# Order of the second scores, the first row sums and v's last cast in batch 0

## The chip, the cores and the metric

The kernel runs on one core of a Trainium2 chip. Its five engines work side by side, each through its own list of instructions in order, and wait for each other by semaphores: TensorE (PE, with its weight loads as PEld), VectorE (DVE), ScalarE (ACT), GpSimd (POOL) and SyncE (SP). The metric is the device time of one execution in microseconds (us), as the median of several runs.

## The reference

```python
k_proj = np.einsum('ks,bhsd->bhkd', E, k)
v_proj = np.einsum('ks,bhsd->bhkd', F, v)
scores = scale * np.matmul(q, k_proj.transpose(0, 1, 3, 2))
scores = scores - np.max(scores, axis=-1, keepdims=True)
attn = np.exp(scores)
attn = attn / (np.sum(attn, axis=-1, keepdims=True) + 1e-09)
attn_out = np.matmul(attn, v_proj).astype(np.float32)
...
x = np.ascontiguousarray(attn_out.transpose(0, 2, 1, 3)).reshape(B * S, H * D)
h1 = x @ w1
h2 = x @ w2
g = np.maximum(h1, h2)
return (g @ w_out).astype(np.float32)
```

There are 8 batches of 8 heads, 1024 positions and 64 dimensions a head. Keys and values are projected from 1024 positions to 64 by E and F, attention runs against these 64, and a layer of 512 to 1024 to 512 with the larger of two products follows on the 8192 rows.

## The kernel before

The kernel takes batch by batch, and each batch in two halves. The heads of a batch form two groups, g=0 (heads 0 to 3) and g=1 (heads 4 to 7), and the positions two halves, j=0 and j=1. A pair (g, j) is one unit of attention: 512 positions of four heads.

The softmax has no maximum; it goes by Exp, row sums, and an inverse made by ACT as the Exp of minus the Ln of the sums. For each unit there are these steps, written as functions in the code:

- `step_sc` (L376): the scores on PE (L340) into a tile of two PSUM banks, and Exp of all 1024 columns on ACT (L380) into `ex`.
- `step_dn` (L382): the row sums, as matmuls of `ex` with ones on PE (L352), into the first half of the same two banks that held the scores; then Ln on ACT (L388) from these banks into `ld`.
- `step_inv` (L425): Exp of minus `ld` on ACT (L427), in place, and a DMA of 8 KB on SP's queue that keeps one row of each inverse in `checked` (L396). `checked` is looked at once, near the end of the kernel, to see whether the sums lay in the range for which this way is exact enough.
- `step_at` (L430): the values on PE (L352), `ex` against the projected v, and two products with the inverse on DVE (L443) that write `xt`, the rows of x, transposed.

`step_kv` (L183) projects k or v. For v it does two heads at a time: 16 matmuls (L195) for each two heads, then one copy of all into `vp` as 16-bit numbers (L207), by DVE or by the engine that is passed as `copy`. With `between` a step is put between the first two heads and the next two.

PSUM has eight banks. Four are single, taken in turn by `mm_bank` (L65). The other four are two tiles of two banks each under the tag `att`, taken in turn by `att_banks` (L71): whoever asks for the third such tile takes the first one's buffer again, and waits until all readers of it are done.

The schedule is manual: each engine's order is the order of the calls. In batch 0, which has no earlier batch to hide its attention behind, the order is written out line by line (L956 to L1005). The part around the change, L984 to L994, before it:

```python
    step_sc(t, 1, 0)
    step_kv(t, 0, 2, "v")
    step_kv(t, 2, 4, "v")
    step_dn(t, 1, 0)
    step_sc(t, 1, 1)
    step_at(t, 0, 0)
    step_at(t, 0, 1)
    step_inv(t, 1, 0)
    step_kv(t, 4, 8, "v", True, copy=nc.scalar.copy, between=lambda: step_dn(t, 1, 1))
    step_inv(t, 1, 1)
    att_banks()
```

The call of `step_kv` for heads 4 to 7 asks for an `att` tile (its fifth argument), puts the second row sums and their Ln between heads 4, 5 and heads 6, 7, and has ACT do the cast. The bare `att_banks()` passes over one buffer in the turn. Behind these lines come `step_wd` (L540: w1 - w2 on DVE, written to `wd_sb`), the values of (1, 0) and (1, 1), and the first matmuls of the up product (`up_slots`, L525), which read `wd_sb` and `xt`; then a transpose of w2 (`step_w2t`, L557) into an `att` tile. The products of `step_at(t, 0, ·)`, which stand earlier, read the inverses of g=0, made well before, and use single banks. The arrival of v is in four DMAs of two heads each.

Of the kernel before, what the change touches and what calls it, by code (L numbers as in the profile page):

```python
# [19 lines left out]
def kernel(  # L20
# [12 lines left out]
    nc = tc.nc  # L33
# [31 lines left out]
    def mm_bank(dtype=FP32, n=None):  # L65
        if n is None:
            n = turn.pop(0)
            turn.append(n)
        return ps.tile([128, 512 if dtype == FP32 else 1024], dtype, tag=f"mm{n}", name="mm_ps")

    def att_banks(dtype=FP32):  # L71
        return ps.tile(
            [128, 2, 512 if dtype == FP32 else 1024], dtype, tag="att", bufs=2, name="att_ps"
        )
# [108 lines left out]
    def step_kv(t, h0=0, h1=H, which="kv", att=False, dma=False, copy=nc.vector.tensor_copy, between=None):  # L183
        kv_ps = att_banks()[:, 0, :] if att else mm_bank(n=0 if dma else None)
        n = (h1 - h0) * D
        both = which == "v"
        nh = 2 if both else h1 - h0
        for h in range(0, h1 - h0, nh):
            if h and between is not None:
                between()  # L190
            for c in range(NC):
                for w in which:
                    i = "kv".index(w)
                    for r in range(2) if both else (i,):
                        nc.tensor.matmul(  # L195
                            out=kv_ps[r * KP : (r + 1) * KP, h * D : (h + nh) * D],
                            lhsT=eft[i][:, c, :],
                            rhs=t[w][:, h0 + h : h0 + h + nh, c, :],
                            start=(c == 0), stop=(c == NC - 1),
                        )  # L200
        zd = lambda ap: ap.rearrange("p (h d z) -> p h z d", d=D // 2, z=2)
        if "k" in which:
            eng = nc.vector.tensor_copy if which == "k" or dma else nc.scalar.copy
            kp = t["kp"][:, h0:h1]
            eng(out=kp[:, :, 0, :], in_=kv_ps[0:KP, 0:n].rearrange("p (h d) -> p h d", d=D))
        if both:
            copy(out=t["vp"][:, h0:h1], in_=zd(kv_ps[:, 0:n]))  # L207
        elif "v" in which:
            def finish_v():
                nc.vector.tensor_copy(out=t["vp"][KP:128, h0:h1], in_=zd(kv_ps[KP:128, 0:n]))  # L210
                if dma:
                    nc.vector.tensor_copy(out=kp[:, :, 1, :], in_=kp[:, :, 0, :])
                    step_kpt_dma(t)
                else:
                    step_vp(t, h0, h1)

            if att:
                return finish_v
            finish_v()


    def step_vp(t, h0=0, h1=H):
        fl = lambda ap: ap[:, h0:h1].rearrange("p h z d -> p (h z d)")
        nc.vector.tensor_copy(out=fl(t["vp"][0:KP]), in_=fl(t["vp"][KP:128]))
# [71 lines left out]
    def step_kpt_dma(t):  # L296
        nc.sync.dma_start_transpose(
            out=t["kpt"], in_=t["kp"].rearrange("p h r d -> p (h r d)")
        )
# [33 lines left out]
    def score(t, g, j, banks):  # L333
        for h in range(2):
            for o in range(2):
                for e in range(2):
                    head = 4 * g + 2 * h + e
                    for s in range(2):
                        pos = D * (o ^ e) + s * Z
                        nc.tensor.matmul(  # L340
                            out=banks[e][pos : pos + Z, h * W : (h + 1) * W],
                            lhsT=kpt_of(t, head, o)[:, s * Z : (s + 1) * Z],
                            rhs=t["qt"][o * D : (o + 1) * D, head, j * W : (j + 1) * W],
                            start=True, stop=True,
                        )
        t["ex", g, j] = soft.tile([128, 2, HALF], FP16, tag="soft", name="ex_sb")
# [12 lines left out]
    def sums_into(t, g, j, dn_ps):  # L359
        tiles_into(lambda o: dn_ps[:, o, :], t["ex", g, j], lambda rows, hh: ones16[rows, 0:Z])  # L360

    def values_into(t, g, j, at_ps):
        for z in range(2):
            tiles_into(
                lambda o: at_ps[o][:, z * W : (z + 1) * W], t["ex", g, j],
                lambda rows, hh: vp_of(t, 4 * g + hh, rows, z),
            )

    def new_xt(t):
        t["xt"] = xpool.tile([128, NP2, 2, HALF], FP16, tag="xt", name="xt_sb")  # L370

    def x_out(t, g, j):
        return t["xt"][:, 2 * g : 2 * g + 2, :, j * W : (j + 1) * W]


    def step_sc(t, g, j):  # L376
        sc_ps = att_banks()
        t["ps", g, j] = sc_ps
        score(t, g, j, [sc_ps[:, e, :] for e in range(2)])
        nc.scalar.activation(out=t["ex", g, j], in_=sc_ps, func=ACTF.Exp, scale=scale)  # L380

    def step_dn(t, g, j):  # L382
        dn_ps = t.pop(("ps", g, j))[:, :, 0:W]
        sums_into(t, g, j, dn_ps)
        ld = (ppool.tile([128, 2, W], FP32, tag="pd", bufs=4, name="ld_sb") if t is tiles[0]
              else soft.tile([128, 2, W], FP32, tag="soft", name="ld_sb"))
        t["ld", g, j] = ld
        nc.scalar.activation(out=t["ld", g, j], in_=dn_ps, func=ACTF.Ln)  # L388
# [4 lines left out]
    def check(inv):  # L393
        rows = checked[4 * n_checked[0] : 4 * n_checked[0] + 4, :]
        n_checked[0] += 1
        nc.sync.dma_start(  # L396
            out=rows, in_=inv.rearrange("(a z) o w -> a z (o w)", z=Z)[:, 0, :]
        )
# [26 lines left out]
    def step_inv(t, g, j):  # L425
        ld = t["ld", g, j]
        nc.scalar.activation(out=ld, in_=ld, func=ACTF.Exp, scale=-1.0)  # L427
        check(ld)

    def step_at(t, g, j, att=False, between=None):  # L430
        if "xt" not in t:
            new_xt(t)
        ld = t.pop(("ld", g, j))
        if att:
            both = att_banks()
            at_ps = [both[:, o, :] for o in range(2)]
        else:
            at_ps = [mm_bank() for _ in range(2)]
        values_into(t, g, j, at_ps)
        for o in range(2):  # L440
            if o and between is not None:
                between()
            nc.vector.tensor_tensor(  # L443
                out=x_out(t, g, j)[:, :, o, :],
                in0=at_ps[o].rearrange("q (z n) -> q z n", z=2),
                in1=ld[:, o, None, :].broadcast_to([128, 2, W]),
                op=ALU.mult,
            )
# [507 lines left out]
    t = tiles[0]  # L956
# [27 lines left out]
    step_sc(t, 1, 0)  # L984
    step_kv(t, 0, 2, "v")
    step_kv(t, 2, 4, "v")
    step_dn(t, 1, 0)
    step_sc(t, 1, 1)
    step_at(t, 0, 0)
    step_at(t, 0, 1)  # L990
    step_inv(t, 1, 0)
    step_kv(t, 4, 8, "v", True, copy=nc.scalar.copy, between=lambda: step_dn(t, 1, 1))
    step_inv(t, 1, 1)
    att_banks()  # L994
    for f0 in (0, 128):
# [85 lines left out]
    t = tiles[1]  # L1081
# [29 lines left out]
    t = tiles[2]  # L1111
# [8 lines left out]
    for b in range(3, B):  # L1120
        t = tiles[b]
# [242 lines left out]
```

## Time and profile before

| | us |
|---|---|
| median of 3 runs | 319.72 (319.67 to 319.75) |
| the profiled execution | 320.29 |
| its span, first to last instruction | 318.5 |
| PE busy in the span | 311.8 (98%) |
| ACT busy in the span | 206.0 (65%) |
| DVE busy in the span | 241.1 (76%) |

The granted clock of TensorE is 1.0 throughout. In the rows of the profile the columns are: start in us from the span's start, duration in us, engine and line, operation, what it writes and reads, the shape, and the number of instructions merged in the row; in square brackets the idle time of the engine ahead of it, and what ended it. A merged row's duration goes from the first start to the last end. Matmuls overlap, so a row of PE can start a little before the row above it ends, and ACT and DVE start an instruction about 0.1 us before the one ahead of it has written its last element. A wait for several semaphores is put down to the one that came last in the profile, which need not be the one that mattered.

### The profile page before, as it was taken

To read this page: it belongs to the slowest core of one execution; us is meant where nothing else is said; L and a number is where in the kernel's file an instruction comes from. 1 tells how busy PE (TensorE), PEld (TensorE's weight loads), DVE (VectorE), ACT (ScalarE), POOL (GpSimd) and SP (SyncE) were. 2 spreads that over 40 slices of the span, in tenths; PEclk is the share of its full clock that TensorE was granted. 3 is DMA by queue.
4 is the path that set the end of the run, shared out by engine and by line. 5 is a ranking of instruction groups with operands and counts; after the bars stand their busy time and mean duration, and the time that the engine had idled before them with its cause. 6 is when DMAs were issued, how large, how long until landed. Compare 5 with 4: busy or idle time off the path is not lost.

```text
span 318.5 us, 9309 instructions
## 1 busy us (share of the span) xinstructions
PE 311.8 (98%) x3922; PEld 253.8 (80%) x3922; DVE 241.1 (76%) x442; ACT 206.0 (65%) x373; POOL 41.4 (13%) x63
## 2 busy tenths in 40 slices
PE   7999999999999999999999999999999999999996
PEld 3565588888887888788887888788887888888885
DVE  2366889887969696896969696996969696969883
ACT  2386742777776777477776777477776777765541
POOL 8259102004000300012000400030000000000000
PEclk9999999999999999999999999999999999999999
DMA  7999999999989999799999999989979131313124
GB/s 179 206 202 197 207 207 201 207 156 141 204 163 183 171 209 245 208 188 147 225 229 219 169 199 245 221 155 174 230 153 217 42 101 36 102 35 102 36 99 136
DMA packets 76684, 53.71 MB, mean 169 GB/s; under 512 B 29664, under 2 KB 76128, under 8 KB 76640
## 3 DMA queue, kind: packets, MB, share of 16 engines
q0 software_dynamic: 30688, 28.05, 56.0%
q1 hardware_dynamic: 45664, 24.85, 33.1%
q8 instruction: 31, 0.51, 0.6%
q10 hardware_dynamic: 288, 0.20, 0.2%
q14 instruction: 13, 0.11, 0.1%
HBM read 57.15 MB, written 16.78 MB: 232 GB/s over the span
## 4 chain that ended last, share of the span: by engine, by line
PE 95%; DMA 3%; ACT 1%; DVE 1%; issue 0%; POOLq 0%
PE mm_ps L838 47%; PE mm_ps L746 27%; PE mm_ps L525 4%; PE mm_ps L195 4%; PE att_ps L352 4%; PE mm_ps L340 2%; DMA k_sb<-in_k_dram 2%; PE mm_ps L634 2%; PE att_ps L237 1%; PE mm_ps L311 1%; PE mm_ps L153 1%; DMA out_dram<-o_sb 1%; PE att_ps L340 0%; DVE qt_sb L316 0%; ACT ld_sb L388 0%
## 5 line engine op out<-in xcount | busy, mean ns | idle before, releaser
L720 ACT COPY p_sb<-mm_ps 128x512 f32<-128x512 f32 x179 | 101.7, 592 | 49.2 <-PE mm_ps L746 27.3
L838 PEld LDWEIGHTS <-big 128*128 128x128 f16 x768 | 73.5, 98 | 11.8 <-issue 3.6
L838 PE MATMUL mm_ps<-T_sb,big 128*128 128x256 f16 x576 | 76.9, 273 | 0.0
L761 DVE TENSOR_TENSOR gt_sb<-mm_ps,p_sb 128x512 f16<-128x512 f32 x56 | 38.5, 688 | 43.0 <-PE mm_ps L746 41.6
L746 PE MATMUL mm_ps<-big,big 128*128 128x256 f16 x336 | 50.4, 273 | 0.0
L746 PEld LDWEIGHTS <-big 128*128 128x128 f16 x448 | 43.8, 98 | 5.1
L838 PE MATMUL mm_ps<-wo_sb,gt_sb 128*128 128x256 f16 x256 | 42.6, 273 | 0.0
L838 PEld LDWEIGHTS <-gt_sb 128*128 128x128 f16 x376 | 35.7, 98 | 6.7 <-issue 2.7
L469 ACT ACTIVATE ex_sb<-mm_ps 128x512 f16<-128x512 f32 x50 | 27.2, 597 | 18.0 <-PE mm_ps L340 12.3
L746 PEld LDWEIGHTS <-wd_sb 128*128 128x128 f16 x336 | 32.9, 98 | 3.8
L746 PE MATMUL mm_ps<-xt_sb,wd_sb 128*128 128x256 f16 x224 | 32.8, 273 | 0.0
L499 DVE TENSOR_TENSOR xt_sb<-att_ps,ld_sb 128x1024 f16<-128x1024 f32 x26 | 31.7, 1219 | 0.2
L303 POOL COPY junk<-qt_sb 1x1 f16<-1x1 f16 x6 | 2.6, 432 | 172.3 <-DMA qt_sb<-q_sb 172.3
L838 PE MATMUL mm_ps<-m_sb,xt_sb 128*128 128x256 f16 x128 | 24.4, 273 | 0.0
L869 DVE TENSOR_TENSOR o_sb<-mm_ps,p_sb 128x512 f32<-128x512 f32 x32 | 21.9, 683 | 2.8 <-ACT p_sb L898 2.0
L764 DVE TENSOR_SCALAR gt_sb<-gt_sb 128x512 f16<-128x512 f16 (+1 forms) x60 | 20.9, 348 | 2.1
L706 DVE TENSOR_TENSOR big<-gt_sb 128x1024 f16<-128x1024 f16 x32 | 21.9, 683 | 0.0
L838 PE MATMUL mm_ps<-wo_sb,big 128*128 128x256 f16 x128 | 21.5, 273 | 0.0
L807 ACT ACTIVATE gt_sb<-mm_ps 128x512 f16<-128x512 f32 x28 | 16.8, 601 | 5.7 <-PE mm_ps L746 5.7
L838 PE MATMUL mm_ps<-T_sb,gt_sb 128*128 128x256 f16 x120 | 20.3, 273 | 0.0
L838 PEld LDWEIGHTS <-xt_sb 128*128 128x128 f16 x188 | 18.3, 98 | 2.3 <-issue 0.2
L761 DVE TENSOR_TENSOR gt_sb<-p_sb 128x512 f16<-128x512 f32 x28 | 19.1, 682 | 0.6 <-ACT p_sb L720 0.6
(121 smaller groups left out, 434.8 us busy)
## 6 DMA issues: line engine op xcount, KB each, us to landing
out_dram<-o_sb SPq DMA_DIRECT2D x62, 256.0 KB
k_sb<-in_k_dram POOLq DMA_DIRECT2D x7, 1024.0 KB, 9.7
v_sb<-in_v_dram POOLq DMA_DIRECT2D x7, 1024.0 KB, 15.4
q_sb<-in_q_dram POOLq DMA_DIRECT2D x5, 1024.0 KB, 22.8
q_sb<-in_q_dram POOLq DMA_DIRECT2D x6, 512.0 KB, 15.9
big<-in_moe_w_dram POOLq DMA_DIRECT2D x12, 128.0 KB, 6.4
v_sb<-in_v_dram POOLq DMA_DIRECT2D x4, 256.0 KB, 14.0
wo_sb<-in_moe_w_out_dram POOLq DMA_DIRECT2D x1, 1024.0 KB, 10.4
```

What stands on the lines that cost most here:

```text
L195: nc.tensor.matmul(out=kv_ps[r * KP : (r + 1) * KP, h * D : (h + nh) * D], lhsT=eft[i][:, c, :], rhs=t[w][:, h0 + h : h0 + h + nh, c, :], ...
L352: nc.tensor.matmul(out=dst(r ^ (hh % 2))[hh * Z : (hh + 1) * Z, :], lhsT=weights(rows, hh), rhs=ex[rows, hh % 2, hh // 2 * W : (hh // 2 + ...
L469: nc.scalar.activation(out=t["ex", g, j][:, e, :], in_=banks[e], func=ACTF.Exp, scale=scale)
L499: nc.vector.tensor_tensor(out=x_out(t, g, j).rearrange("q z o n -> q o z n"), in0=at_ps.rearrange("q o (z n) -> q o z n", z=2), in1=ld[:, ...
L706: nc.vector.tensor_tensor(out=S(i), in0=S(0) if x is None else x, in1=y(), op=op)
L720: copy(out=x, in_=bank)
L746: nc.tensor.matmul(out=bank[:, m * W : (m + 1) * W], lhsT=w_[:, n_, (2 * d + m) * 128 : (2 * d + m + 1) * 128], rhs=a[:, n_, :], start=(n ...
L761: nc.vector.tensor_tensor(out=c_blk(j, c), in0=two(x), in1=two(y), op=ALU.add)
L764: nc.vector.tensor_scalar_max(ap, ap, 0.0)
L807: nc.scalar.activation(out=out, in_=in_, func=ACTF.Relu)
L838: nc.tensor.matmul(out=bank[i][:, 0:CH] if two_banks else bank[:, i * CH : (i + 1) * CH], lhsT=a(c)[:, i * 128 : (i + 1) * 128], rhs=w_(c) ...
L869: nc.vector.tensor_tensor(out=o_sb, in0=two(x), in1=two(y), op=ALU.add)
```

## The change

```diff
     step_sc(t, 1, 0)
     step_kv(t, 0, 2, "v")
     step_kv(t, 2, 4, "v")
+    step_sc(t, 1, 1)
     step_dn(t, 1, 0)
-    step_sc(t, 1, 1)
     step_at(t, 0, 0)
     step_at(t, 0, 1)
+    step_kv(t, 4, 8, "v", True, copy=nc.scalar.copy, between=lambda: step_dn(t, 1, 1))
     step_inv(t, 1, 0)
-    step_kv(t, 4, 8, "v", True, copy=nc.scalar.copy, between=lambda: step_dn(t, 1, 1))
     step_inv(t, 1, 1)
     att_banks()
```

The scores of (1, 1) and their Exp come ahead of the row sums of (1, 0) and their Ln. The projection of v for heads 4 to 7, with the second row sums, their Ln and the cast, comes ahead of the inverse of (1, 0), so that both inverses stand behind the cast. On PE the order turns from sums, scores, values, v, sums, v into scores, sums, values, v, sums, v. On ACT it turns from Exp(1,0), Ln(1,0), Exp(1,1), inverse(1,0), Ln(1,1), cast, inverse(1,1), into Exp(1,0), Exp(1,1), Ln(1,0), Ln(1,1), cast, inverse(1,0), inverse(1,1). DVE's order stays. SP's two DMAs to `checked` keep their order and go out when their inverses are done. The order of buffers under the tag `att` stays too: scores of (1, 0), scores of (1, 1), v, one passed over, values of (1, 0), values of (1, 1).

## The prediction

> **What bounds the kernel now.** I read the page first: busy time of each engine and the chain of waits by engine. Then I asked for PE's waits alone, from 24 us to the end.
>
> ```profile
> PE 311.8 (98%) x3922; PEld 253.8 (80%) x3922; DVE 241.1 (76%) x442; ACT 206.0 (65%) x373; POOL 41.4 (13%) x63
> PE 95%; DMA 3%; ACT 1%; DVE 1%; issue 0%; POOLq 0%
> ```
>
> ```profile
> PE mm_ps L1196 <- DMA out_dram<-o_sb: 1.2, 1, 1.2
> ```
>
> The last row is the only wait of PE after 24 us, and it stands at the very end, behind a store. So from 24 us on TensorE sets the pace without a pause: what reaches PE late before that point should be paid in full at the end of the kernel. The other engines appear on the chain for 1% each, and the question is only where. The chain in order of time, from 17 to 26 us, answers it:
>
> ```profile
> 18.84 1.20 PE mm_ps L195 x32
> 20.04 0.29 PE att_ps L352 x8
> 20.36 0.60 ACT ld_sb L388
> 20.95 0.91 ACT ex_sb L380
> 21.87 0.52 ACT ld_sb L427
> 22.38 0.50 ACT ld_sb L388
> 22.89 0.33 ACT vp_sb L207
> 23.25 0.63 PE att_ps L352 x32
> 23.89 1.83 PE mm_ps L525 x8
> ```
>
> From 20.36 to 23.25 us, 2.9 us, the chain runs through ACT, and these are the very operations that the change reorders. By this view alone one would take the inverse (L427, 0.52 us) out of the chain and promise half a microsecond. A chain names one releaser per step, however, so I laid the two engines beside each other, ACT first (start, duration):
>
> ```profile
> 18.91 1.02 ACT L380 ACTIVATE ex_sb<-att_ps 128x1024 f16<-128x1024 f32 x1 [0.57 <-PE att_ps L340]
> 20.36 0.60 ACT L388 ACTIVATE ld_sb<-att_ps 128x512 f32<-128x512 f32 x1 [0.42 <-PE att_ps L352]
> 20.85 1.02 ACT L380 ACTIVATE ex_sb<-att_ps 128x1024 f16<-128x1024 f32 x1
> 21.75 0.63 ACT L427 ACTIVATE ld_sb<-ld_sb 128x512 f32<-128x512 f32 x1
> 22.29 0.60 ACT L388 ACTIVATE ld_sb<-att_ps 128x512 f32<-128x512 f32 x1
> 22.83 0.37 ACT L207 CAST vp_sb<-att_ps 128x256 f16<-128x256 f32 x1
> 23.10 0.63 ACT L427 ACTIVATE ld_sb<-ld_sb 128x512 f32<-128x512 f32 x1
> ```
>
> ```profile
> 18.43 0.41 PE L340 MATMUL att_ps<-qt_sb,kpt_sb 64*32 64x256 f16 x16
> 18.77 1.27 PE L195 MATMUL mm_ps<-v_sb,eft 128*64 128x128 f16 x32
> 19.98 0.30 PE L352 MATMUL att_ps<-ex_sb,ones 64*32 64x256 f16 x8
> 20.09 0.41 PE L340 MATMUL att_ps<-qt_sb,kpt_sb 64*32 64x256 f16 x16
> 20.31 0.74 PE L352 MATMUL mm_ps<-ex_sb,vp_sb 64*32 64x256 f16 x32
> 21.00 0.64 PE L195 MATMUL att_ps<-v_sb,eft 128*64 128x128 f16 x16
> 21.92 0.30 PE L352 MATMUL att_ps<-ex_sb,ones 64*32 64x256 f16 x8 [0.28 <-ACT ex_sb L380]
> 22.15 0.64 PE L195 MATMUL att_ps<-v_sb,eft 128*64 128x128 f16 x16
> 23.25 0.63 PE L352 MATMUL att_ps<-ex_sb,vp_sb 64*32 64x256 f16 x32 [0.47 <-ACT vp_sb L207]
> 23.82 1.90 PE L525 MATMUL mm_ps<-xt_sb,wd_sb 128*128 128x512 f16 x8
> 25.55 0.61 PE L557 MATMUL att_ps<-ident,big 128*128 128x128 f16 x8
> ```
>
> Read across, in four links. PE's second row sums (21.92) start 0.05 us behind the end of the second Exp (20.85 + 1.02 = 21.87). The second Ln (22.29) starts 0.07 behind those sums' end (21.92 + 0.30), so the inverse at 21.75 hardly held it up. The cast of v (22.83) starts 0.04 behind the end of v's second half on PE (22.15 + 0.64 = 22.79), so the cast isn't held by ACT at all. And the values (23.25) start 0.05 behind the cast. What sets the time of the cast is therefore the row of PE work: v's first half at 21.00, the sums at 21.92, the second half at 22.15.
>
> **What the change does to this.** Nothing is added or removed: the same matmuls, activations and DMAs run in another order. There are two moves.
>
> The second move, the inverse of j=0 behind the cast (0.63 us of ACT, about 0.5 as a step between its neighbours), frees ACT between 21.75 and 22.29. I cost this at nothing: both instructions that follow it waited for PE, by the links above. Its other end needs a look, since the inverse is now late for the product on DVE that reads it:
>
> ```profile
> 23.81 1.29 DVE L443 TENSOR_TENSOR xt_sb<-att_ps,ld_sb 128x512 f16<-128x512 f32 x2
> ```
>
> This product starts 0.98 behind the cast's start (22.83), which is 0.56 behind the start of the values on PE (23.25). With the inverse behind the cast, the inverse starts 0.27 after the cast's start (as 23.10 follows 22.83), ends 0.63 later, at cast + 0.90, and with a semaphore's 0.05 the product could start at cast + 0.95. The values still decide, by 0.03 us. Were the inverse 0.1 later than this, the product would be too, and PE would not notice: its next reader of the freed bank is a transpose 1.73 us behind the start of L525 (25.55 against 23.82), while the product's pair ends at 23.81 + 1.29 = 25.10, 0.45 us ahead. The inverse also sends 8 KB to `checked` on SP's queue:
>
> ```profile
> 17.85 6.41 SPq L396 DMA_DIRECT2D checked<-ld_sb  x4
> ```
>
> SP issues nothing else between 17 and 62 us, and `checked` is read only near the end of the kernel, so the later DMA costs nothing.
>
> The first move is the one that costs. PE now runs the second scores ahead of the first sums, and so ACT's order turns from Exp, Ln, Exp into Exp, Exp, Ln. The second Exp gains, the first Ln loses. Who waits for that Ln? The `att` tag has two buffers. The first scores take one, the second scores the other, and the v projection of heads 4 to 7 asks for a third: it takes the first one's, where the first row sums have just been written, and must wait until Ln has read them. In the profile of before that wait can barely be seen: Ln ends at 20.36 + 0.60 = 20.96, v's first half starts at 21.00, and PE itself was busy until about then with the values (20.31 + 0.74 = 21.05). Now for the sum, step by step.
>
> ```profile
> 19.40 0.48 PEld L195 LDWEIGHTS <-eft 128*64 128x64 f16 x16 [0.15 <-DMA v_sb<-in_v_dram]
> 21.57 0.09 PEld L352 LDWEIGHTS <-ones 64*32 64x32 f16 x1
> ```
>
> 1. Second scores on PE. They follow v's heads 0 to 3, which end at 18.77 + 1.27 = 20.04. The change from such matmuls to small tiles is shown by the weights of the sums: loaded at 21.57, 0.07 ahead of the end of v's first half (21.64). So the scores start at 19.97 instead of 20.09.
> 2. Second Exp: scores to Exp took 18.91 - 18.43 = 0.48, so it starts at 20.45 instead of 20.85.
> 3. First Ln: an Exp of this size hands ACT on after 21.75 - 20.85 = 0.90, so Ln starts at 21.35 instead of 20.36, and ends 0.60 later, at 21.95.
> 4. v's first half: 0.05 behind it, at 22.00 instead of 21.00. Here 1.00 us is lost.
> 5. Second sums: the Exp that they waited for until 21.87 now ends at 21.47, so they follow v's first half at once, 0.57 behind its start (21.00 to 21.57): 22.57 instead of 21.92. Of the 1.00 us, the 0.35 us that PE had waited here is won back.
> 6. From there everything keeps its distances. Sums to cast is 0.91 (21.92 to 22.83), and the second Ln fits in: it starts 0.37 behind the sums and hands on 0.49 later (20.36 to 20.85), at 0.86. Cast at 23.48 instead of 22.83, values at 23.90, L525 at 24.47 instead of 23.82.
>
> The sum is 0.57 + 22.00 - 21.92 = **0.65 us later**, and by the first view it stays to the end. The profiled execution took 320.29 us, of which the span is 318.5; it would take 320.94. The median of the runs, 319.72, is 0.57 below the profiled one, and the same step on it gives 320.37 us.
>
> **Unknown costs.** Step 1 depends on a landing: PE's weights at 19.40 waited 0.15 us for heads 2 and 3 of v. A run in which these land earlier lets the second scores start up to 0.15 sooner, down to the end of the first Exp on ACT. Before, that bought nothing, as the first sums waited for that same Exp (18.91 + 1.02 = 19.93, sums at 19.98); now it goes straight into step 3. Bound below: 0.65 - 0.15 = 0.50. A later landing moves both kernels alike. Bounds above: DVE's first product starts at 20.97 and is put down to that first Ln.
>
> ```profile
> 20.97 2.49 DVE L443 TENSOR_TENSOR xt_sb<-mm_ps,ld_sb 128x512 f16<-128x512 f32 x4 [0.60 <-ACT ld_sb L388]
> 23.37 0.48 DVE L541 TENSOR_TENSOR wd_sb<-big,big 128x256 f16<-128x256 f16 x2
> ```
>
> By the code these products read the inverses of heads 0 to 3, long done, and the values, 0.66 earlier on PE (20.31); I take the latter, and the Ln (ending at 20.96) for a coincidence. If they did wait for it, they would start at 21.96, the first half of `wd_sb` would be ready at 21.96 + (23.37 - 20.97) + 0.24 (half of the pair's 0.48) = 24.60, and L525 would start there instead of 24.47: 0.78 in all. If an Exp handed on only at its end (1.02, not 0.90), 0.12 more; between rows of two decimals and the tile changes I allow 0.05 either way.
>
> **Rivals.** (a) The landing comes early in ordinary runs: +0.50 to 0.60, 320.22 to 320.32. For it: the wait of 0.15 is there, so there is something to win. Against: the trace shows one execution, and no row says that it lands sooner in others. (b) Faster: v's first half doesn't wait for the first Ln. It would run at 21.00 as now, the second sums would follow at 21.57 instead of 21.92, since Exp is done by 21.47, and the cast would start at 22.48: 0.35 us won, 319.37. It decides if the start at 21.00 came from PE's own work (the values to 21.05) and not from Ln's end at 20.96; the trace of before can't separate the two. Against it stand the two `att` buffers in the code. (c) PE's clock falls because PE pauses longer: between the end of the values near 21.0 and 22.00 it is now idle for about 1 us.
>
> ```profile
> 1.47 3.43 PE L153 MATMUL mm_ps<-ones 128*128 128x512 f16 x8 [1.47 <-DVE ones L146]
> 8.57 1.03 PE L195 MATMUL mm_ps<-k_sb,eft 128*64 128x256 f16 x8 [1.04 <-DMA k_sb<-in_k_dram]
> 14.33 1.06 PE L195 MATMUL mm_ps<-k_sb,eft 128*64 128x256 f16 x8
> ```
>
> At the start eight matmuls of 512 columns took 3.43 us; the eight of L525 take 1.90. At the slow pace L525 would cost 1.5 us more: +2.15, 321.87. Against it: after a pause of 1.04 us at 8.57 eight matmuls took 1.03 us, and the same eight in the middle of work 1.06, so a pause of this length did not slow PE. The Trainium skill, TensorE: Matmul & The Clock Gate, section "Part 1: The HAM clock gate", puts the fall at an idle window of about 3.4 us, while "A second HAM failure mode: psum-queue depth-cycling" says that many short idles between groups can bring it too. By the first rule nothing happens here, by the second this rival would; the row at 8.57 agrees with the first. (d) No effect: PE after 24 us has hidden room, and the delay is swallowed, 319.72. The single wait after 24 us speaks against it.
>
> **Chances.** The forecast (+0.60 to 0.90) has 0.68, (a) 0.16, (b) 0.05, (c) 0.06, (d) 0.05. A measurement of this kernel tells about 0.2% from no change, 0.64 us, 320.36; the forecast sits just above that line. Of its 0.68 I put 0.60 above, since all open bounds but the landing lie upward, and 0.08 below. Slower: 0.60 + 0.06 = 0.66. Within 0.2%: 0.08 + 0.16 + 0.05 = 0.29. Faster: 0.05. The range takes in the forecast and (a): from 0.50 less 0.05, and some 0.04 for the spread of the runs, 320.13, to 0.78 + 0.12 plus the same, 320.71. (b), (c) and (d), 0.16, are left out.
>
> **What would show it.** In the profile after: the second Exp near 20.45 and the first Ln ending near 21.95; v's first half 0.05 behind it, near 22.00, with a wait of PE for Ln of about 0.9 us that was not there; second sums without their wait of 0.28; cast near 23.48; L525 near 24.47; and no new wait of PE after it. If v's first half starts at 21.0, (b) holds; if L525's eight take over 3 us, (c); if L525 is late by 0.65 but the span isn't, (d). If the second scores start before 19.95, it is (a).

## The result and the profile after

The changed kernel takes 320.68 us as the median of nine runs (320.21 to 321.4), against 319.75 for nine runs of the kernel before. The ratio is 1.0027, with a 95% interval of 1.0016 to 1.0037: 0.5 to 1.2 us slower. 320.37 had been forecast, from 320.13 to 320.71. The profiled execution took 321.17 us, its span 319.4.

Two lines of the page, and three of PE's waits in the whole span:

```profile
span 319.4 us, 9309 instructions
...
PE 95%; DMA 3%; ACT 1%; DVE 1%; SPq 0%; issue 0%
```

```profile
PE mm_ps L1196 <- DMA out_dram<-o_sb: 1.2, 1, 1.2
PE att_ps L195 <- ACT ld_sb L388: 1.0, 1, 1.0
PE att_ps L352 <- ACT vp_sb L207: 0.5, 1, 0.5
```

The second row is new: the first half of v's heads 4 to 7 (L195; called v's half from here on) waits 1.0 us for a Ln (L388). The wait of 0.28 us for the second Exp is gone. Asked from 25 us to the end, PE's only wait is still the one for a store, the first row. ACT and PE around the change, in order of time (start, duration):

```profile
20.66 1.02 ACT L380 ACTIVATE ex_sb<-att_ps 128x1024 f16<-128x1024 f32 x1 [0.33 <-PE att_ps L340]
21.58 0.59 ACT L388 ACTIVATE ld_sb<-att_ps 128x512 f32<-128x512 f32 x1
23.17 0.60 ACT L388 ACTIVATE ld_sb<-att_ps 128x512 f32<-128x512 f32 x1 [0.99 <-PE att_ps L352]
23.70 0.37 ACT L207 CAST vp_sb<-att_ps 128x256 f16<-128x256 f32 x1
23.97 1.15 ACT L427 ACTIVATE ld_sb<-ld_sb 128x512 f32<-128x512 f32 x2
```

```profile
18.82 0.41 PE L340 MATMUL att_ps<-qt_sb,kpt_sb 64*32 64x256 f16 x16
19.16 1.08 PE L195 MATMUL mm_ps<-v_sb,eft 128*64 128x128 f16 x32
20.18 0.41 PE L340 MATMUL att_ps<-qt_sb,kpt_sb 64*32 64x256 f16 x16
...
22.22 0.64 PE L195 MATMUL att_ps<-v_sb,eft 128*64 128x128 f16 x16 [0.96 <-ACT ld_sb L388]
22.79 0.30 PE L352 MATMUL att_ps<-ex_sb,ones 64*32 64x256 f16 x8
23.02 0.64 PE L195 MATMUL att_ps<-v_sb,eft 128*64 128x128 f16 x16
24.13 0.63 PE L352 MATMUL att_ps<-ex_sb,vp_sb 64*32 64x256 f16 x32 [0.47 <-ACT vp_sb L207]
24.69 1.90 PE L525 MATMUL mm_ps<-xt_sb,wd_sb 128*128 128x512 f16 x8
```

The first Ln ends at 21.58 + 0.59 = 22.17, and v's half starts at 22.22. ACT then stands idle for 0.99 us while PE does the work that it had done under ACT's cover before. The up matmuls (L525) start at 24.69 instead of 23.82, 0.87 later. Not all of this is the change. This execution reached the first scores of heads 4 to 7 at 18.82 instead of 18.43, by code that is the same in both kernels: its first projection of k on PE had started at 8.96 instead of 8.57, the same 0.39 later, behind a copy of k that ACT began at 8.29 instead of 6.41, when k's first DMA was in. And heads 2 and 3 of v caused no wait in it. The two traces therefore have to be compared from an event behind that accident and ahead of the change's effect. The end of v's heads 2 and 3 on PE is one: 20.04 before (18.77 + 1.27), 20.24 after (19.16 + 1.08). From there to the up matmuls it is 3.78 us before and 4.45 after. I call this distance the yardstick. From the up matmuls to the end of the span it is 294.7 us in both.

### The profile page after: what moved, and what is told of

Its sections match the earlier page's. It is cut to its first block, busy times and chain, and to the rows that moved or that the text cites. A ratio compares the mean times of both kernels' runs of the same rounds, so it can differ in the third digit from the quotient of the medians.

```text
span 319.4 us, 9309 instructions
## 1 busy us (share of the span) xinstructions
PE 312.1 (98%) x3922; PEld 253.9 (79%) x3922; DVE 240.9 (75%) x442; ACT 206.1 (65%) x373; POOL 40.3 (13%) x63
## 4 chain that ended last, share of the span: by engine, by line
PE 95%; DMA 3%; ACT 1%; DVE 1%; SPq 0%; issue 0%
PE mm_ps L838 47%; PE mm_ps L746 27%; PE mm_ps L525 4%; PE mm_ps L195 4%; PE att_ps L352 4%; PE mm_ps L340 2%; DMA kf_sb<-in_k_dram 2%; PE mm_ps L634 2%; PE att_ps L237 1%; PE mm_ps L311 1%; PE mm_ps L153 1%; DMA out_dram<-o_sb 1%; PE att_ps L340 1%; DVE qt_sb L316 0%; ACT ld_sb L388 0%; PE mm_ps L167 0%
```

## The experiments

The first four expectations that follow still use the first scores as their zero, the later ones the end of v's heads 2 and 3. This table has all runs by the second, with the stretch from the up matmuls to the end of the span, the median, and the ratio to runs of the kernel before that were taken beside them. Their medians were 319.75 us beside the changed kernel, 319.78 beside the next four rows, 319.81 beside the four after these and 319.93 beside the last. The ratio is not the quotient of the two medians, and can differ from it by up to 0.1%.

Two rows need care. In "scores ahead of v's heads 2 and 3" and in "Exp in halves" the second scores stand ahead of the zero and push it back (by 0.34 us in the latter, from 18.50 to 18.84), so their 3.67 and 3.68 must not be set beside 3.78. From the first scores they have 5.56 and 5.57, against 5.39 before and 5.87 changed.

| run | yardstick | stretch to the end | median us | ratio, 95% interval |
|---|---|---|---|---|
| before | 3.78 | 294.7 | | |
| changed | 4.45 | 294.7 | 320.68 | 1.0027 (1.0016 to 1.0037) |
| scores ahead, alone | 4.44 | 294.7 | 320.41 | 1.0020 (1.0011 to 1.0029) |
| inverse behind, alone | 3.77 | 294.7 | 319.82 | 1.0002 (0.9993 to 1.0011) |
| v in a single bank | 4.15 | 295.5 | 321.12 | 1.0044 (1.0031 to 1.0058) |
| scores ahead of v's heads 2 and 3 | 3.67 | 294.7 | 319.89 | 1.0008 (0.9999 to 1.0017) |
| changed, again | 4.44 | 294.7 | 320.53 | 1.0029 (1.0008 to 1.0050) |
| single bank, turn kept | 4.15 | 294.7 | 320.12 | 1.0003 (0.9984 to 1.0023) |
| copy ahead of Ln | 4.96 | 294.7 | 320.90 | 1.0040 (1.0024 to 1.0057) |
| copy ahead of the inverses | 4.44 | 295.1 | 320.97 | 1.0037 (1.0022 to 1.0051) |
| Exp in halves | 3.68 | 295.3 | 320.34 | 1.0005 (0.9990 to 1.0020) |

### Each move alone

First the scores, with the inverse where it was:

```diff
+    step_sc(t, 1, 1)
     step_dn(t, 1, 0)
-    step_sc(t, 1, 1)
...
     step_inv(t, 1, 0)
     step_kv(t, 4, 8, "v", True, ...)
```

> The first move alone: the second scores ahead of the first row sums, the first inverse left ahead of v's last half. Yardstick in the trace: from the start of the first scores of heads 4 to 7 to the start of the first up matmuls (L525); 5.39 us in the kernel before (18.43 to 23.82), 5.87 in the changed one (18.82 to 24.69). Theory (v's half waits for a Ln that now comes after both Exps): all of the loss is here. The inverse fits on ACT between the first Ln and the second sums, so the yardstick is 5.87 to 6.05 and the time 0.5 to 0.9 us over before, as in the changed kernel. Rival (the loss comes from the cast and the inverses): yardstick 5.4, time within 0.2 us of before.

PE's rows of v's heads 2 and 3, of v's half and of the up matmuls in this run, and one of ACT:

```profile
18.50 1.27 PE L195 MATMUL mm_ps<-v_sb,eft 128*64 128x128 f16 x32 [0.21 <-DMA v_sb<-in_v_dram]
...
21.75 0.64 PE L195 MATMUL att_ps<-v_sb,eft 128*64 128x128 f16 x16 [0.96 <-ACT ld_sb L388]
...
24.21 1.90 PE L525 MATMUL mm_ps<-xt_sb,wd_sb 128*128 128x512 f16 x8
```

```profile
21.73 0.63 ACT L427 ACTIVATE ld_sb<-ld_sb 128x512 f32<-128x512 f32 x1
```

The yardstick is 24.21 - 19.77 = 4.44, the changed kernel's to 0.01, with the same wait of 0.96 us for Ln. The inverse at 21.73 lies inside ACT's idle time. From the first scores it is 6.35 us, outside the 5.87 to 6.05 that I had written, since here v landed late against the scores. That miss was one of the yardstick, and led to the new one. The time is 0.63 us over before. The first move alone is enough for the whole of the local delay.

Then the second move alone:

```diff
+    step_kv(t, 4, 8, "v", True, copy=nc.scalar.copy, between=lambda: step_dn(t, 1, 1))
     step_inv(t, 1, 0)
-    step_kv(t, 4, 8, "v", True, copy=nc.scalar.copy, between=lambda: step_dn(t, 1, 1))
     step_inv(t, 1, 1)
```

> The second move alone: both inverses behind v's cast, scores and sums in the old order. Theory: the instructions that stood behind the first inverse on ACT waited for PE anyway, and the inverse is back just in time for its product, so yardstick (first scores of heads 4 to 7 to L525) 5.39 as before, time within 0.15 us of before. Rival from the chain of waits (the inverse's 0.52 us is on the path): yardstick 4.9, 0.5 us faster. Other rival (the late inverse holds up DVE): L525 starts as before, but the transposes behind it wait, 0.1 to 0.5 us slower.

```profile
18.93 0.64 PE L195 MATMUL mm_ps<-v_sb,eft 128*64 128x128 f16 x16 [0.29 <-DMA v_sb<-in_v_dram]
...
20.52 0.64 PE L195 MATMUL att_ps<-v_sb,eft 128*64 128x128 f16 x16
21.43 0.30 PE L352 MATMUL att_ps<-ex_sb,ones 64*32 64x256 f16 x8 [0.28 <-ACT ex_sb L380]
...
23.34 1.90 PE L525 MATMUL mm_ps<-xt_sb,wd_sb 128*128 128x512 f16 x8
```

v's half doesn't wait, the sums wait 0.28 us for the second Exp as before, and the yardstick is 23.34 - 19.57 = 3.77. From the first scores (17.37) it is 5.97 and not the 5.39 that I had written, again because v landed late. The time can't be told from before. So the inverse's 0.52 us in the chain of waits of before was no half microsecond to be had: taken off ACT's path, it changed nothing.

### Another wait in the place of the one for Ln

```diff
-    step_kv(t, 4, 8, "v", True, copy=nc.scalar.copy, between=lambda: step_dn(t, 1, 1))
+    step_kv(t, 4, 8, "v", copy=nc.scalar.copy, between=lambda: step_dn(t, 1, 1))
     step_inv(t, 1, 0)
     step_inv(t, 1, 1)
-    att_banks()
```

> The changed order, but v's heads 4 to 7 go to a single PSUM bank instead of the pair that the first row sums still occupy: the wait for Ln is gone, in its place stands one for DVE's first product, which frees that bank (21.66 in the trace before). Theory: v's half starts about 3.3 us after the first scores (18.43 to 21.71) instead of 3.40 to 3.57 behind the Ln, the yardstick is about 5.75 where v's second quarter lands late and 5.6 where it lands early, time 0.2 to 0.4 us over before. If the wait for Ln isn't what costs: yardstick as in the changed kernel, 5.87.

The yardstick came near what was expected, 4.15 instead of 4.45 (5.80 from the first scores), but the time was 1.34 us over before. PE's waits behind 25 us show a second one in this run:

```profile
PE mm_ps L1195 <- DMA out_dram<-o_sb: 1.2, 1, 1.2
PE mm_ps L634 <- ACT gt_sb L534: 0.7, 1, 0.7
```

Taking one more single bank had turned the order of the banks, and the product of the weights (L634), which asks for fixed banks, now met one that a Relu on ACT was still reading. The stretch to the end is 0.8 us longer for it. So I put the turn back:

```diff
     step_kv(t, 4, 8, "v", copy=nc.scalar.copy, between=lambda: step_dn(t, 1, 1))
+    turn.insert(0, turn.pop())
```

> As the run with v in a single bank, but with the turn of the banks put back behind it, so that the product of the weights finds its bank free as before (there it had waited 0.7 us for a Relu). Theory: yardstick from the end of v's heads 2 and 3 is 4.14 as there (1.66 to 5.80 behind the first scores), the stretch to the end is 294.7 again, time 0.36 us over before. If the rotation of banks wasn't what cost there: stretch to the end 295.5 again, time over 1 us over before.

```profile
17.99 1.33 PE L195 MATMUL mm_ps<-v_sb,eft 128*64 128x128 f16 x32 [0.30 <-DMA v_sb<-in_v_dram]
...
21.00 0.64 PE L195 MATMUL mm_ps<-v_sb,eft 128*64 128x128 f16 x16 [0.67 <-DVE xt_sb L443]
...
23.47 1.90 PE L525 MATMUL mm_ps<-xt_sb,wd_sb 128*128 128x512 f16 x8
```

v's half waits 0.67 us for DVE's first product instead of 0.96 for Ln. The yardstick is 23.47 - 19.32 = 4.15, 0.30 under the changed kernel's, and the stretch to the end is 294.7 again. The median lies 0.31 over before; the interval is too wide to tell that from nothing, so it is the trace that decides here. ACT's activations stand in the changed kernel's order, and yet the yardstick shrank by 0.30, as the wait did by 0.29. So the wait for the banks, and not the order of the activations as such, carries this part of the loss; the 0.37 that is left goes with the new wait of 0.67.

### The second Exp earlier still

```diff
     step_kv(t, 0, 2, "v")
-    step_kv(t, 2, 4, "v")
     step_sc(t, 1, 1)
+    step_kv(t, 2, 4, "v")
     step_dn(t, 1, 0)
```

> The changed order with the second scores one step earlier still, ahead of v's heads 2 and 3. Theory: the second Exp follows the first at once (0.92 behind its start instead of 1.36 to 1.54), so the first Ln ends 0.45 to 0.6 earlier, v's half starts at about 2.95 us after the first scores, the second sums at 3.5 (3.49 in the kernel before), yardstick 5.4 to 5.5: the loss is nearly gone, time within 0.25 us of before. Nothing here depends on when v's second quarter lands. Rival (the loss is the two Exps in a row, or the late inverses): yardstick 5.87 or more, time like the changed kernel's.

In this run's profiled execution TensorE's granted clock was 0.50 from 10 to 15 us and 1.00 again from 16 us on, and PE reached the first scores 2.8 us late, at 21.19. Only distances behind them are read; they lie at full clock.

```profile
21.67 1.94 ACT L380 ACTIVATE ex_sb<-att_ps 128x1024 f16<-128x1024 f32 x2 [0.57 <-PE att_ps L340]
23.50 0.60 ACT L388 ACTIVATE ld_sb<-att_ps 128x512 f32<-128x512 f32 x1
```

```profile
24.15 0.64 PE L195 MATMUL att_ps<-v_sb,eft 128*64 128x128 f16 x16
24.72 0.30 PE L352 MATMUL att_ps<-ex_sb,ones 64*32 64x256 f16 x8
```

```profile
26.41 0.48 DVE L541 TENSOR_TENSOR wd_sb<-big,big 128x256 f16<-128x256 f16 x2
```

The two Exps run back to back, Ln ends 2.91 us behind the first scores (21.19) instead of 3.35, and v's half starts at 2.96 instead of 3.40; the profile shows no wait of PE there. The time is 0.11 us over before, inside what can't be told apart. Two Exps in a row and late inverses therefore cost little, as long as Ln comes early enough: 0.17 us from the first scores to the up matmuls (5.56 against 5.39), where the changed kernel's first trace has 0.48. The up matmuls come at 5.56 (26.75), a little over my 5.4 to 5.5: the differences of the weights, which DVE made from 26.41 on, two in 0.48, were the last thing ready, and the profile names them for the weight load of L525.

### One cost doubled, in two places

A copy of 128x512 on ACT, whose output nobody reads, was put into the changed kernel, once ahead of the first Ln and once ahead of the inverses, with the changed kernel itself beside them.

```diff
+    spare = opool.tile([128, 2 * DM // 2], FP32, tag="o", name="o_sb")
     step_sc(t, 1, 0)
...
     step_sc(t, 1, 1)
+    nc.scalar.copy(out=spare, in_=ones16)
     step_dn(t, 1, 0)
```

> The changed kernel once more, beside the next three. New yardstick, since the first profiles showed that v's landings move against the first scores: from the end of v's heads 2 and 3 on PE to the start of the first up matmuls; 3.78 us before (20.04 to 23.82), 4.45 changed (20.24 to 24.69). Theory: 4.45 again, v's half 0.05 behind the first Ln, time 0.5 to 0.7 us over before. Rival (something besides the local delay, since the first runs stood 0.93 us apart and the delay is 0.48 to 0.67): 0.8 us or more over before, and a stretch from the first up matmuls to the end longer than the 294.7 us of the kernel before.

> The changed kernel with one more copy of 128x512 on ACT (output unused) between the second Exp and the first Ln. Theory: the first Ln sets the time of v's half, and that of everything behind it, so a delay of about 0.5 us goes through in full: PE waits 0.5 us longer for Ln, yardstick 4.45 + 0.5 = 4.95, time 0.5 us over the changed kernel. Rival (v's half isn't bound by this Ln): yardstick 4.45, time as the changed kernel.

The run with the copy ahead of Ln, ACT and PE:

```profile
21.92 0.61 ACT L989 CAST o_sb<-ones 128x512 f32<-128x512 f16 x1
22.42 0.60 ACT L388 ACTIVATE ld_sb<-att_ps 128x512 f32<-128x512 f32 x1
```

```profile
19.94 0.64 PE L195 MATMUL mm_ps<-v_sb,eft 128*64 128x128 f16 x16 [0.34 <-DMA v_sb<-in_v_dram]
...
23.08 0.64 PE L195 MATMUL att_ps<-v_sb,eft 128*64 128x128 f16 x16 [1.48 <-ACT ld_sb L388]
...
25.54 1.90 PE L525 MATMUL mm_ps<-xt_sb,wd_sb 128*128 128x512 f16 x8
```

The copy held Ln back by 0.50 us (21.92 to 22.42). PE's wait grew from 0.96 to 1.48, and the yardstick from 4.44 to 25.54 - 20.58 = 4.96: the delay goes through in full to the up matmuls, and the stretch behind them is unchanged. The medians differ by 0.37, with intervals too wide to say more. The changed kernel itself stood 0.72 us over before this time, just above the 0.5 to 0.7 that I had expected, with the yardstick and the stretch to the end unchanged. So the 0.93 of the first comparison needs no cause besides the delay: 0.67 lies inside both intervals (0.51 to 1.18 and 0.26 to 1.60 us).

> The changed kernel with the same copy on ACT placed between v's cast and the two inverses. Theory: the inverse is back just in time for its product, and PE has 0.2 to 0.45 us of room behind it; so the yardstick stays at 4.45, the products on DVE come 0.45 to 0.5 later, and PE waits 0.1 to 0.3 us at the transposes behind them: time 0.1 to 0.3 us over the changed kernel. Rival (the late inverses are part of what the change costs): the whole 0.5 us is added.

The run with the copy ahead of the inverses, PE and DVE:

```profile
23.78 1.90 PE L525 MATMUL mm_ps<-xt_sb,wd_sb 128*128 128x512 f16 x8
25.68 0.61 PE L557 MATMUL att_ps<-ident,big 128*128 128x128 f16 x8
...
27.21 0.61 PE L557 MATMUL att_ps<-ident,big 128*128 128x128 f16 x8
```

```profile
24.24 1.29 DVE L443 TENSOR_TENSOR xt_sb<-att_ps,ld_sb 128x512 f16<-128x512 f32 x2 [1.09 <-ACT ld_sb L427]
...
25.78 1.28 DVE L443 TENSOR_TENSOR xt_sb<-att_ps,ld_sb 128x512 f16<-128x512 f32 x2
```

The second pair of products and the second transposes in the kernel before:

```profile
25.35 1.28 DVE L443 TENSOR_TENSOR xt_sb<-att_ps,ld_sb 128x512 f16<-128x512 f32 x2
```

```profile
26.86 0.61 PE L557 MATMUL att_ps<-ident,big 128*128 128x128 f16 x8
```

The up matmuls keep their place (yardstick 4.44). DVE's product comes 0.46 behind them, where it starts with them in the changed kernel, and the first transposes (L557) start 1.90 behind them instead of 1.73 (23.82 to 25.55 before). The second transposes start 1.53 behind the first (25.68 to 27.21), instead of 1.31 (25.55 to 26.86). Together PE loses 0.17 + 0.22 = 0.39 us, which is the 0.4 by which the stretch to the end grows, more than the 0.1 to 0.3 that I had expected; the medians differ by 0.44. So of the 0.46 us on the products only 0.07 is hidden. The changed kernel doesn't need that room: its product comes no later behind the values than before (0.55 against 0.56), and its stretch to the end is that of before.

### An order for both sides

Ln waits behind an Exp of 1024 columns that could be cut. In this run the second Exp is two of 512, one ahead of the first Ln and one behind. To use what that frees, the differences of the weights go ahead of DVE's fourth product, and the up matmuls of j=0 ahead of those of j=1.

```diff
     step_kv(t, 0, 2, "v")
+    halves = step_sc_halves(t, 1, 1)
+    halves(0)
     step_kv(t, 2, 4, "v")
-    step_sc(t, 1, 1)
     step_dn(t, 1, 0)
+    halves(1)
     step_at(t, 0, 0)
-    step_at(t, 0, 1)
+    step_at(t, 0, 1, between=lambda: [step_wd(f0, 0, 2, 128) for f0 in (0, 128)])
...
-    for i in range(2):
-        for u in u0, u1:
+    for u in u0, u1:
+        for i in range(2):
             u[i](r1=2)
```

> An order that gives both sides what they need: the second scores ahead of v's heads 2 and 3, their Exp cut in two halves of 512 columns, one ahead of the first Ln, where ACT sat idle, and one behind it; the first two differences of weights on DVE one product earlier, and the up matmuls of j=0 ahead of those of j=1. Theory: the first Ln comes as early as before the change (0.3 us behind the end of v's heads 2 and 3), the second half of the Exp ends 0.5 us earlier than the whole did, the second sums follow v's half without their wait, the cast comes 0.3 us earlier than before, and the yardstick is 3.45 if the first differences of weights are ready, up to 3.8 where their weights land late (at 22.9 to 23.0 us in the traces): time 0 to 0.3 us under before. Rival (the wait for the second Exp wasn't what PE waited for): yardstick 3.78 or more, time as before or slower.

```profile
22.82 0.49 DVE L548 TENSOR_TENSOR wd_sb<-big,big 128x256 f16<-128x256 f16 x2 [0.51 <-DMA big<-in_moe_w_dram]
```

```profile
23.16 1.90 PE L532 MATMUL mm_ps<-xt_sb,wd_sb 128*128 128x512 f16 x8
25.25 0.61 PE L564 MATMUL att_ps<-ident,big 128*128 128x128 f16 x8 [0.19 <-DVE xt_sb L450]
```

(Lines from L382 on are 7 higher in this kernel.) DVE now stands 0.51 us waiting for the weights' DMA, the up matmuls come at 23.16, 3.68 behind v's heads 2 and 3, and the products that DVE put off make the transposes late: the stretch to the end is 295.3, 0.6 more. Nothing is won: the median is 0.41 over before, not 0 to 0.3 under as expected, though by the ratio it can't be told from before. This run moves several things at once, so it doesn't separate them. As far as these runs show, the stretch is bounded from three sides at nearly the same time: ACT's row of activations, DVE's row of products, and the landings of v and of the first weights. No version that I ran beats the kernel before.

## Why the prediction was right

Sign and mechanism held, and so did the size of the local delay. By its own steps, all taken from the end of v's heads 2 and 3 in the changed kernel's first trace (20.24):

| step | by the prediction's distance | measured |
|---|---|---|
| 1, second scores, 0.07 ahead of that end | 20.17 | 20.18 |
| 2, second Exp, 0.48 later | 20.66 | 20.66 |
| 3, first Ln, 0.90 later | 21.56 | 21.58 |
| 3, end of Ln, 0.60 later | 22.18 | 22.17 |
| 4, v's half, 0.05 later | 22.22 | 22.22 |
| 5, second sums, 0.57 later, no wait | 22.79 | 22.79 |
| 6, cast, 0.91 later | 23.70 | 23.70 |
| 6, up matmuls, 0.99 later | 24.69 | 24.69 |

Each distance is counted from the measured row above it. The sum was 0.65; the yardsticks differ by 0.67.

The open cost on the lower side was real. In the changed kernel's first trace v was there in time, and measured from the first scores the loss is 5.87 - 5.39 = 0.48, just under the bound of 0.50 that I had put on it. So locally this trace is the case of rival (a): its second scores start 1.36 us behind the first, where the forecast had 1.54. The reason that I gave, that an early v buys nothing in the old order because the first sums wait for the first Exp anyhow, is argued: no trace of the old order has v in time. In the profiles of the run with the scores alone and of the repeated changed kernel v was waited for on PE (0.21 us, and 0.26), and the yardsticks say 0.66 in both. So the loss of one execution lies, by these traces, between 0.48 and 0.67 with the landing. The times scatter more than that. The changed kernel's medians were 0.93 and 0.72 over before, that of the scores alone 0.63, with the local delay inside each interval. The first of these lies only 0.03 us inside the upper end of the range, and that it fell inside was partly luck: nothing in the sum explains the 0.28 between 0.93 and 0.65.

The costs named on the upper side did not come true. DVE's first product did not wait for the first Ln:

```profile
21.18 2.48 DVE L443 TENSOR_TENSOR xt_sb<-mm_ps,ld_sb 128x512 f16<-128x512 f32 x4 [0.60 <-PE mm_ps L352]
...
24.68 1.29 DVE L443 TENSOR_TENSOR xt_sb<-att_ps,ld_sb 128x512 f16<-128x512 f32 x2 [0.62 <-ACT ld_sb L427]
```

It starts at 21.18, 1 us ahead of that Ln's end, and the profile now names the values. The attribution of before (to Ln) was the coincidence that I had taken it for. The second row answers to the inverse's margin of 0.03 us: the product that I had due 0.56 behind the values (24.13) starts 0.55 behind them, and is put down to the inverse. In the run with the scores alone this inverse is long done (21.73 + 0.63), and yet the product starts 0.56 behind the values (23.65 to 24.21), after 0.62 us of idle time on DVE. So the values decide there, the two are level in the changed kernel, and nothing is lost by it. But the room that I had given behind this product, 0.45 us, was far too large. In the run with the copy ahead of the inverses the first transposes, which write into the freed bank, start 0.15 behind the end of the products (24.24 + 1.29 = 25.53 to 25.68). I had left this out; with it the room there was 0.30. And I had left the second pair out. Before, its products end at 25.35 + 1.28 = 26.63 and the second transposes start at 26.86; less the same 0.15, the room was 0.08, and that agrees with the 0.07 that the copy left hidden. An inverse 0.1 us later than in the changed kernel would by these rows have begun to cost time. That the second move cost nothing rests on the near tie of inverse and values, and little on the room behind it.

Of the rivals, the clock (c) fell: the eight up matmuls take 1.90 us behind a wait of 0.96, and again 1.90 in the run with the copy ahead of Ln, behind one of 1.48. Rival (b) fell with the wait for Ln, which is in every trace of this order; and its price was probably wrong too. It held that a cast 0.35 us earlier would bring the end forward by as much, with the up matmuls at 23.47. But in the trace before DVE only starts the differences of the weights at 23.37, two in 0.48, and in the run with the Exp in halves, where they come earlier, DVE waits for the weights' landing. The price of that rival had left this out. Rival (d), that the delay is swallowed, fell with the stretch to the end, 294.7 in both kernels.

## What to carry to other kernels

When two engines hand work to and fro, the name in the chain is the last releaser, not the thing to take away: ask for each instruction on it what it waited for, and for each that is moved back who waits for its buffer. A wait that ends at the same moment as the engine's own work can't be seen in a trace, and appears in full once its releaser moves. Where the start of a kernel wanders from run to run, choose a zero behind the wandering part, and count from there.

## What the runs showed of the hardware

A row that moved without a cause in the code: the first scores of heads 4 to 7 lay at 18.43 us in the profile of before, at 18.82 in that of the changed kernel, and at 17.49 in its repetition, while the end of v's heads 2 and 3 lay at 20.04, 20.24 and 19.44. PE's early work follows the first landings. The wait for v, where there is one, takes up part of the difference: the 0.94 us between 18.43 and 17.49 are 0.60 at the end of heads 2 and 3.

A pause of PE of 1.48 us, in the run with the copy ahead of Ln, left its granted clock at full speed. One of 1.68 us near the start of the run with the scores ahead of v's heads 2 and 3 was followed by a fall:

```profile
8.95 1.73 PE L195 MATMUL mm_ps<-k_sb,eft 128*64 128x256 f16 x8 [1.68 <-ACT k_sb L961]
```

These eight matmuls took 1.03 us in the changed kernel's trace. The granted clock here was 1.00 up to 9 us, 0.50 from 10 to 15 and 1.00 again from 16 us on. That the pause brought the fall is not shown: one of 1.49 us in the same place, in the run with the copy ahead of Ln, brought none. The Trainium skill, TensorE: Matmul & The Clock Gate, section "Part 1: The HAM clock gate", gives about 3.4 us of idling for a fall. The pauses of 1.48 and 1.49 us agree with that; the fall behind 1.68 us does not, and here the measurement decides. So the margin against rival (c) was smaller than the prediction's rows made it look.

Ahead of matmuls of a larger tile shape the loader of the weights stands idle, and no wait explains it. Two such rows in the changed kernel, the last one the weights of the up matmuls:

```profile
20.41 0.57 PEld L352 LDWEIGHTS <-vp_sb 64*32 64x32 f16 x32
21.19 0.11 PEld L195 LDWEIGHTS <-eft 128*64 128x64 f16 x1 [0.21 <-issue]
...
24.69 1.41 PEld L525 LDWEIGHTS <-wd_sb 128*128 128x128 f16 x8 [0.21 <-issue]
```

At 21.19 the shape turns from 64*32 to 128*64, at 24.69 from 64*32 to 128*128, and both times the loader was idle for 0.21 us with no releaser named. At 24.69 DVE had ended the differences of the weights at 23.58 + 0.48 = 24.06. The Trainium skill, TensorEngine Tiling (Array Packing), section "Key Properties", says that a change of tiling mode drains the engine, without a figure. The rows fit that, but no run here separates such a drain from other causes, and how much of the 0.21 us PE itself loses is not shown.
